# Feed-forward of an FNet + GEGLU block: 1024 tokens per first block, hidden values by way of DRAM, down projection spread over two quarters

## The chip, the cores and the metric

The kernel runs on one core of a Trainium2 chip. The metric is device time in microseconds (us): the median of several executions of the whole kernel. Engines are named as in the profile: PE (TensorE matmul) with PEld (its weight loads), DVE (VectorE), ACT (ScalarE), POOL (GpSimd), and SP, whose queue issues nearly all DMAs. Each engine works through its own queue strictly in order; an instruction that waits holds everything queued behind it.

## The reference

x has 2048 tokens of 448 values. A layer norm is followed by a Fourier mixing layer (real part of a DFT over the hidden axis and the sequence axis), added to x; then a second layer norm and a gated feed-forward with 1792 hidden values, added again:

```
h  = x + A(layernorm(x))           # a = x Wd_re^T, b = x Wd_im^T; A = Ws_re a - Ws_im b
g, u = layernorm(h) @ w_gate, layernorm(h) @ w_up
out = h + (gelu(g) * u) @ w_down
```

All arrays are float32. The kernel multiplies in float16 and splits each operand into a high and a low half (hi + lo), so that one product is three float16 products.

## The kernel before

**Stages.** The DFT over the sequence and over the hidden axis comes first and ends, on PE, at 346 us. While it runs, DVE and ACT also split all 14 blocks of gate and up weights (class `Weights`: `sums`, `split`) and store them to `w_dram`. The feed-forward starts then. Its matrix products are cut by Strassen's scheme: seven block products instead of eight, with sums of operand blocks made before (on DVE or POOL) and sums of results after.

**Gate and up (class `GateUp`, L1022).** The tokens are four quarters q of 512; by Strassen a product's moving operand has half of them, `TQ = 256` columns. For each quarter there are 14 steps f (`NF`), so t runs from 0 to 55. A step is 39 matmuls in seven products: x1, y1, x2, z1, y2, z2, y3 (L1040 to L1072), accumulated in three PSUM banks X, Y, Z. Between products other engines read a bank: ACT copies X into Y after x1 (L1043), takes u2 from Y after y1 (L1048), the gelu g1 from X after x2 (L1053), m5 from Z after z1 (L1059); DVE takes one "plus" each from Y after y2, from Z after z2 (both L1010) and from Y after y3 (L1072). `c_last` then takes a second gelu (ACT) and a multiplication on POOL (L1081). The results lie in `hh`, in SBUF, for two quarters at a time.

**Down.** d counts 56 pieces: 8 groups p of 128 tokens times 7 pieces of the hidden axis. Before piece d is used, `dn_sums` (L1121) makes sums on POOL (two) and DVE (one), `dn_hi` (L1132) two ACT copies, `dn_lo` (L1137) two DVE subtractions; then `dn_mm` runs 21 matmuls of 224 columns. After 7 pieces a `Drain` (L908) brings the group's four PSUM banks home: two copies on ACT, four additions on DVE from PSUM, eight additions on POOL (L954), a store.

**Order of the work.** Everything is ordered by hand, in the loop over t (L1260). Quarter 0 has gate and up alone, and beside it the down weights are split (`down_prep`, L967: `down_sums` on POOL, `down_hi` on ACT, `down_lo` on DVE, one n of 7 per two steps); the last two `hid_mm` of the DFT (21 matmuls each) run in it as well. From t = 14 on each step takes one d, for 42 steps; the other 14 pieces (groups 6 and 7) run in a tail after t = 55, eight of them split early (`EARLY`, L1095). The layer norm and the operand splitting of quarters 2 and 3 are laid over the steps of quarters 1 and 2 (table at L1210). Split weights are read back from `w_dram` each step (896 KB).

Of the kernel before, what the change touches and what calls it, by code (L numbers as in the profile page):

```python
# [13 lines left out]
P = 128  # L14
# [18 lines left out]
def kernel(  # L33
# [46 lines left out]
    fops = ctx.enter_context(tc.tile_pool(name="fops", bufs=1))  # L80
    dram = ctx.enter_context(tc.tile_pool(name="dram", bufs=1, space=bass.MemoryType.DRAM))
# [92 lines left out]
    hops = {}  # L174
# [3 lines left out]
    def hops_tile(q):  # L178
        hops[q] = ring.tile([P, N_OPS, 2 * P], F16, tag="ops", bufs=2, name=f"hops{q}")
# [22 lines left out]
    def down_load(n):  # L202
        wd32[n] = fops.tile([P, 4, HD], F32, tag="xn" if n % 2 else "tt", name=f"wd32_{n}")
        nc.sync.dma_start(wd32[n].rearrange("p (k c) d -> p k (c d)", k=2), w_down[n])
# [16 lines left out]

    def ffn_norm_act(q, j, h):

        tag = f"h{q}_{j}"
        mv, r = moments.pop((q, j))
        xn = fops.tile([P, 2, D], F32, tag="xn", name=f"xn_{tag}")

        nb = mv[:, :, 1]
        V.scalar_tensor_tensor(nb, mv[:, :, 0], -1.0, r, op0=ALU.mult, op1=ALU.mult)
# [57 lines left out]
    def ffn_transpose(q, j, parts):  # L287
        xs = ffn[q, j][2]
        ops = hops[q]
        for n in parts:  # L290
            s0, s1 = ((0, 8), (8, 16), (16, 22), (22, 25))[n]
            nc.sync.dma_start_transpose(ops[:, s0:s1, j * P : (j + 1) * P], xs[:, s0 * P : s1 * P])


    for q in range(2):
        hops_tile(q)
# [7 lines left out]
    class Weights:  # L304


        def __init__(self, f):
            self.f = f
            self.raw = dft.tile([P, 2, 6, P], F32, tag="raw", bufs=2, name=f"gu_raw{f}")
# [3 lines left out]
        def sums(self):  # L313
            gate, up = self.raw[:, 0], self.raw[:, 1]
            s = self.s = dft.tile([P, 10, P], F32, tag="s", name=f"gu_s{self.f}")
# [19 lines left out]
        def split(self, of_raw):  # L335
            if of_raw:
                self.w = w_tile(f"gu_w{self.f}")
            for s0, s1, src in self.parts(of_raw):
                hi_part(self.slots(0, s0, s1, src), src, W_SC)
            for s0, s1, src in self.parts(of_raw):  # L340
                lo_part(self.slots(1, s0, s1, src), src, self.slots(0, s0, s1, src), W_SC)

# [105 lines left out]
    def fast_sums(n):  # L448
        fast_s[n] = dft.tile([P, 8 * P], F32, tag="wr", bufs=5, name=f"sums{n}")
        fast_w[n] = [dft.tile([P, 2, 8 * P], F16, **place, name=f"ws{n}_{k}") for k, place in enumerate(fast_places(n))]  # L450
# [5 lines left out]

    def fast_places(n):
        ring = dict(tag="ws", bufs=6)
        return (dict(tag="raw", bufs=2), ring) if n == FAST + 2 else (ring, ring)
# [54 lines left out]
    def fast_out(n, k):  # L514

        sc = 1.0 / (X_SC * D_SC)
        if k == 1:

            e = dft.tile([P, 10, P], F32, tag="s", name=f"e{n}")
# [44 lines left out]
    def t_tile(j):  # L564
# [11 lines left out]
        if j == 7:  # L576
            return dft.tile([P, 4 * D], F16, tag="raw", bufs=2, name="t7")
# [76 lines left out]
    def wh_load(n):  # L654

        k0, k1 = WH[n]
        t = wh_raw[n] = dft.tile([P, k1 - k0, D], F32, tag="raw", bufs=2, name=f"wh_raw{n}")
# [49 lines left out]
    gu = {}  # L707

# [9 lines left out]
    for k, f in enumerate(reversed(range(NF))):  # L718
        n = (17, 20, 22, 25, 27, 30, 33, 35, 38, 40, 43, 45, 48, 50)[k]
# [72 lines left out]
    for n in range(N_STEPS):  # L792
# [89 lines left out]
        for half in range(2):  # L882
# [4 lines left out]
            for what in after.get((n, half), ()):  # L887
                what()
    z_turn(NP - 1)
    down_sums(0)  # L890

# [7 lines left out]
    gw_first = fpool.tile([P, 4, 28 * P], F16, tag="hh", bufs=2, name="gw_first")  # L899

    def gw_first_load(t, queue=nc.sync):

        gw[t] = gw_first[:, (t - 3) % 7, :]
        queue.dma_start(gw[t], w_dram[t])

    gw_first_load(4)
# [56 lines left out]
    def down_lo(n, k):  # L963
        dst, src = down_parts(n)[k]
        lo_part(wd[n][:, 1, dst], src, wd[n][:, 0, dst], W_SC)

    def down_prep(t, part=None):  # L967

        n, odd = divmod(t, 2)
        if odd and part != 1:  # L970
            if n < NC:
                down_lo(n, 1)
                if n + 2 < NC:
                    down_load(n + 2)
            if n + 1 < NC:
                down_sums(n + 1)
        elif not odd and n < NC:
            if part != 1:
                down_hi(n, 0)
                down_lo(n, 0)  # L980
            if part != 0:
                down_hi(n, 1)
# [3 lines left out]
    TQ = 2 * P  # L986

    def product(ps, q, t, a, b, first, last):

        w, ops = gw[t].rearrange("p (l o d) -> p l o d", l=2, o=14), hops[q]  # L990
# [20 lines left out]

    def ftile(tag, bufs, name, n=TQ):
        return fpool.tile([P, n], F32, tag=tag, bufs=bufs, name=name)

    hh = {}

    def f_of(t):

        q, f = divmod(t, NF)
        return f if q < 3 else f // 2 + f % 2 * (NF // 2)  # L1020

    class GateUp:  # L1022


        def __init__(self, t):
            self.t, self.name = t, f"{t}"
            self.q, self.f = t // NF, f_of(t)

            self.own = self.q > 0 or t % 2 == 0

        def bank(self, k):
            pool, tag = (ps_gu, "XYZ"[k]) if self.own else (ps_dn, f"a{k}")
            if self.q > 0 and k == 1 and self.t % 2:
                pool, tag = ps_tr, "tr"
            return pool.tile([P, 512], F32, tag=tag, name=f"p{'XYZ'[k]}_{self.name}")[:, :TQ]

        def mul(self, ps, a, b, first):
            product(ps, self.q, self.t, a, b, first, True)

        def x1(self):  # L1040
            self.X, self.Y = self.bank(0), self.bank(1)
            self.mul(self.X, "A11", "B11", True)
            A.activation(self.Y, self.X, AF.Copy)  # L1043

        def y1(self):
            self.mul(self.Y, "S2", "T2", False)
            self.u2 = ftile("u2", 2, f"u2_{self.name}")
            A.activation(self.u2, self.Y, AF.Copy, scale=SC)  # L1048

        def x2(self):  # L1050
            self.mul(self.X, "A12", "B21", False)
            self.g1 = ftile("g1", 2, f"g1_{self.name}")
            A.activation(self.g1, self.X, AF.Gelu_apprx_tanh, scale=1.0 / (X_SC * W_SC))  # L1053

        def z1(self):
            self.Z = self.bank(2)
            self.mul(self.Z, "S1", "T1", True)
            self.m5 = ftile("m5", 1, f"m5_{self.name}")
            A.activation(self.m5, self.Z, AF.Copy, scale=SC)  # L1059

        def y2(self):
            self.mul(self.Y, "S3", "T3", False)
            plus(self.hidden(1), self.Y, self.m5)

        def z2(self):
            self.mul(self.Z, "S4", "B22", False)
            self.c12 = ftile("c12", 2, f"c12_{self.name}")
            plus(self.c12, self.Z, self.u2)

        def y3(self):  # L1070
            self.mul(self.Y, "A22", "T4", False)
            V.scalar_tensor_tensor(self.hidden(0), self.Y, SC, self.g1, op0=ALU.mult, op1=ALU.mult)  # L1072

        def hidden(self, g):
            k, n = divmod(self.f, NF // 2)
            return hh[self.q][:, n, 2 * k + g, :]

        def c_last(self):
            A.activation(self.c12, self.c12, AF.Gelu_apprx_tanh, scale=1.0 / H_SC)  # L1079
            c22 = self.hidden(1)  # L1080
            G.tensor_mul(c22, c22, self.c12)  # L1081
# [6 lines left out]
    NC = NF // 2  # L1088
    dn_s, dn_w, acc_d, hr = {}, {}, {}, {}

    def dn_hid(d):
        p, n = divmod(d, NC)
        return hh[p // 2][:, n, :, p % 2 * P : (p % 2 + 1) * P]

    EARLY = [42, 43, 49, 44, 45, 50, 46, 47]  # L1095
    EARLY_AT = dict(zip((44, 46, 47, 48, 50, 51, 52, 54), EARLY))

    def dn_tile(d):

        def tile(pool, tag, bufs, n=14 * P):  # L1100
            return pool.tile([P, n], F16, tag=tag, bufs=bufs, name=f"dn_w{d}")

        if d in EARLY:
            k = EARLY.index(d)
            if k < 3:
                if k == 0:
                    dn_w["early"] = tile(ring, "ops", 2, N_OPS * 2 * P)
                w = dn_w["early"][:, k * 14 * P : (k + 1) * 14 * P]
            elif k < 6:
                w = tile(fops, ("xs", "xn", "tt")[k - 3], 1)  # L1110
# [335 lines left out]
```

## Time and profile before

| | us |
|---|---|
| median of 3 runs | 723.15 (723.01 to 725.27) |
| the profiled execution, its own time | 723.14 |
| its span, first to last instruction | 721.3 |
| first matmul of the feed-forward | 346.0 |
| first matmul of the down projection | 420.8 |
| last matmul | 717.9 |

The granted TensorE clock is 1.000 throughout. In the profile a row of the timeline has the start (us from the span's start), the duration, the engine, the source line, the operation, out<-in, the shape and a count of merged instructions; a bracket tells how long the engine sat idle before it and what released it. Rows grouped by line have the busy time and the mean ns of one instruction. Instructions of one engine follow each other a little closer than their durations say: the distance of two starts is the price, the duration is latency.

### The profile page before, as it was taken

The page shows a single profiled execution, that of the slowest core. Times are in us where ns is not written, and L with a number is a line of the kernel's source. Part 1 is how long each engine was busy: PE and PEld are TensorE (multiplying, and loading weights), DVE is VectorE, ACT ScalarE, POOL GpSimd, SP SyncE. Part 2 cuts the span into 40 slices and gives each one's busy share as a digit, 9 for nine tenths or more (in the row PEclk, how much of TensorE's full clock was granted, in tenths as well). Part 3 has the DMA queues.
Part 4 walks back from the last instruction along what each step waited for, and adds up shares of the span by engine and source line. Part 5 has one row for each costly group of instructions (what it writes and reads, how often), then busy time and mean ns, then how long its engine had stood idle before and what let it go on. Part 6 is the DMA issues. An engine that isn't in the chain of part 4 may idle for free.

```text
span 721.3 us, 14165 instructions
## 1 busy us (share of the span) xinstructions
PE 706.4 (98%) x5496; PEld 533.4 (74%) x5496; DVE 518.2 (72%) x1063; ACT 366.3 (51%) x726; POOL 190.8 (26%) x250
## 2 busy tenths in 40 slices
PE   9999999999999999999999999999999999999897
PEld 5555555555555555898778899899998999999896
DVE  7997639596959889998644567686586765667594
ACT  5776525254436655442637655554555544465431
POOL 0000000000000000000435643363453635657473
PEclk9999999999999999999999999999999999999999
DMA  8787549999999999572787325558466585444301
GB/s 268 248 249 258 130 161 272 260 333 276 250 352 287 287 292 263 190 182 92 213 318 281 130 94 157 180 180 224 156 174 178 183 222 176 160 141 165 129 20 60
DMA packets 101588, 147.70 MB, mean 205 GB/s; under 512 B 60944, under 2 KB 72336, under 8 KB 101520
## 3 DMA queue, kind: packets, MB, share of 16 engines
q1 hardware_dynamic: 101376, 145.88, 66.7%
q8 instruction: 43, 0.70, 0.4%
q10 hardware_dynamic: 144, 0.92, 0.4%
q14 instruction: 25, 0.20, 0.1%
HBM read 112.69 MB, written 20.19 MB: 184 GB/s over the span
## 4 chain that ended last, share of the span: by engine, by line
PE 90%; DVE 3%; ACT 3%; POOL 2%; DMA 1%; issue 1%; ACTq 0%; SPq 0%; DVEq 0%; POOLq 0%
PE acc L626 33%; PE pY L1000 13%; PE acc_d L1171 12%; PE y L691 9%; PE pZ L1000 8%; PE pX L1000 8%; PE acc_f L498 7%; DVE dn_w L111 2%; DMA gw<-w_dram 1%; ACT wd L107 1%; POOL hr L954 1%; ACT xn_h L231 1%; DVE wd L113 0%; POOL dn_s L1125 0%; POOL dn_s L1126 0%
## 5 line engine op out<-in xcount | busy, mean ns | idle before, releaser
L626 PE MATMUL acc<-xs,ws 128*128 128x448 f16 x1248 | 237.9, 352 | 0.3 <-DVE xs L148 0.3
L626 PEld LDWEIGHTS <-ws 128*128 128x128 f16 x1248 | 122.1, 98 | 114.3 <-issue 0.4
L1000 PEld LDWEIGHTS <-gw 128*128 128x128 f16 x1755 | 171.3, 98 | 22.4 <-issue 2.9
L1171 PE MATMUL acc_d<-wd,dn_w 128*128 128x224 f16 x1176 | 133.4, 259 | 3.3 <-ACT v L922 3.3
L1171 PEld LDWEIGHTS <-dn_w 128*128 128x128 f16 x1176 | 113.2, 98 | 6.6 <-issue 3.8
L1000 PE MATMUL pY<-hops,gw 128*128 128x256 f16 x765 | 105.2, 273 | 2.1 <-ACT u L1048 1.5
L209 POOL TENSOR_TENSOR wd_s<-wd 128x448 f32<-128x448 f32 x7 | 7.9, 1132 | 353.9 <-DVE r_h L141 342.1
L113 DVE SCALAR_TENSOR_TENSOR ws<-wr,ws 128x1024 f16<-128x1024 f32 (+2 forms) x66 | 75.0, 1139 | 6.6 <-ACT ws L107 6.6
L107 ACT ACTIVATE ws<-wr 128x1024 f16<-128x1024 f32 (+2 forms) x66 | 64.4, 980 | 29.6 <-DMA wr<-in_w_seq_dram 28.6
L1081 POOL TENSOR_TENSOR hh<-hh,c 128x256 f32<-128x256 f32 x56 | 45.5, 812 | 115.5 <-ACT c L1079 115.5
L1000 PE MATMUL pX<-hops,gw 128*128 128x256 f16 x495 | 68.8, 273 | 2.1 <-DMA gw<-w_dram 2.1
L1000 PE MATMUL pZ<-hops,gw 128*128 128x256 f16 x495 | 68.7, 273 | 0.0
L691 PE MATMUL y<-wh,z 128*128 128x448 f16 x336 | 66.2, 352 | 0.0
L1048 ACT ACTIVATE u<-pY 128x256 f32<-128x256 f32 x56 | 21.4, 382 | 79.7 <-PE pY L1000 79.6
L1125 POOL TENSOR_TENSOR dn_s<-hh 128x256 f32<-128x256 f32 x56 | 44.1, 788 | 48.9 <-DVE dn_w L111 48.8
L1010 DVE SCALAR_TENSOR_TENSOR hh<-pY,m 128x256 f32<-128x256 f32 x56 | 23.6, 421 | 43.7 <-PE pY L1000 41.3
L691 PEld LDWEIGHTS <-z 128*128 128x128 f16 x336 | 32.9, 98 | 29.6
L111 DVE TENSOR_TENSOR dn_w<-dn_s,dn_w 128x640 f16<-128x640 f32 x56 | 52.6, 940 | 1.4 <-ACT dn_w L107 1.4
L1010 DVE SCALAR_TENSOR_TENSOR c<-pZ,u 128x256 f32<-128x256 f32 x56 | 23.8, 424 | 37.3 <-PE pZ L1000 34.8
L498 PEld LDWEIGHTS <-ws 128*128 128x128 f16 x504 | 48.3, 98 | 0.9
L1126 POOL TENSOR_TENSOR dn_s<-hh 128x256 f32<-128x256 f32 x56 | 48.8, 871 | 0.0
L107 ACT ACTIVATE dn_w<-dn_s 128x640 f16<-128x640 f32 x56 | 40.8, 729 | 13.5 <-POOL dn_s L1126 7.9
(117 smaller groups left out, 874.6 us busy)
## 6 DMA issues: line engine op xcount, KB each, us to landing
gw<-w_dram SPq DMA_DIRECT2D x45, 896.0 KB, 4.7
wr<-in_w_seq_dram SPq DMA_DIRECT2D x100, 256.0 KB, 5.1
w_dram<-gu_w SPq DMA_DIRECT2D x14, 896.0 KB, 7.1
gu_raw<-in_w_gu_dram SPq DMA_DIRECT2D x28, 384.0 KB, 6.2
wr<-in_w_seq_dram SPq DMA_DIRECT2D x14, 512.0 KB, 5.6
gw_first<-w_dram SPq DMA_DIRECT2D x7, 896.0 KB, 6.2
x<-in_x_dram SPq DMA_DIRECT2D x16, 224.0 KB, 3.3
hx<-in_x_dram SPq DMA_DIRECT2D x8, 448.0 KB, 6.6
```

Of the source, the lines that this page charges most:

```text
L107: A.activation(dst, src, AF.Copy, scale=scale)
L111: V.tensor_sub(dst, src, hi)
L113: V.scalar_tensor_tensor(dst, src, scale, hi, op0=ALU.mult, op1=ALU.subtract)
L498: PE.matmul(fast_sum(n, k), fast_a(n, i, lw, a), fast_b(j, lx, b), start=j == 0 and m == 0 and k % 2 == 0, stop=j == NT // 2 - 1 and m == ...
L626: PE.matmul(acc[key][:, :D], w[:, lw, block * P : (block + 1) * P], xs[c][:, lx, :], start=c == 0 and m == 0, stop=c == NT - 1 and m == 2,)
L691: PE.matmul(y[:, :D], z[p][:, lz, k, g * P : (g + 1) * P], wh[:, lw, k, :], start=k == 0 and m == 0, stop=k == 6 and m == 2,)
L1000: PE.matmul(ps, w[:, wl, wa + ws, :], ops[:, m + ms, :], start=first and n == 0, stop=last and n == len(terms) - 1, skip_group_check=True,)
L1010: V.scalar_tensor_tensor(dst, ps, SC, other, op0=ALU.mult, op1=ALU.add)
L1081: G.tensor_mul(c22, c22, self.c12)
L1125: G.tensor_add(s[:, 0:2], t[:, 0:2], t[:, 2:4])
L1126: G.tensor_sub(s[:, 2:4], t[:, 1:4:2], t[:, 0:4:2])
L1171: PE.matmul(ps, w[:, la, a, :], wd[n][:, lb, b, :], start=n == 0 and m == 0 and opens, stop=n == NC - 1 and m == 2, skip_group_check=True,)
```

## The change

Quarters 0 and 1 become one block of 1024 tokens (`block_of(t) == 0`, t = 0 to 13) whose matmuls have 512 moving columns. Quarters 2 and 3 are blocks 1 and 2 (t = 14 to 41) with 256 columns as before. All 56 pieces of the down projection stay; the 42 that lie beside gate and up are spread over the 28 steps of blocks 1 and 2, one or two per step (`COUNT`), and 12 pieces of the last two groups are split in block 2 too (`EARLY`, one per step from t = 30), which leaves two splits to the tail.

Of the gate and up weights only six blocks (13, 12, 11, 0, 1, 2) are split during the DFT; blocks 3 to 10 (`JIT_F`) are split in steps 1 to 8 of block 0, each two steps ahead. The splitting of the down weights is moved into steps 0 to 5 (n = 0 and 1 in step 0, then one per step). The two last `hid_mm` both run in step 1. Hidden values go from a ring of three tiles (`hs`) to DRAM (`hid_dram`) and come back piece by piece (`hid_load`), except those of block 2's last two groups, which are used from SBUF. The bias of the second layer norm is a step of its own (`ffn_bias`), ahead of `ffn_norm_act`. The tiles with the tags `raw` and `s` move from the pool `dft` to a pool `prep` that stays open.

```diff
+    DFT_F = ((13, 20), (12, 25), (11, 30), (0, 45), (1, 48), (2, 50))
+    JIT_F = range(3, 11)
...
-        q, f = divmod(t, NF)
-        return f if q < 3 else f // 2 + f % 2 * (NF // 2)
+    N_GU = 3 * NF
+        self.n = 4 * P if self.block == 0 else 2 * P
...
+        def store(self):
+            k, n = divmod(self.f, NC)
+            if self.block == 0:
+                nc.sync.dma_start(hid_dram[0, n][:, :, 2 * k : 2 * k + 2], hs[self.t].rearrange(...))
+            else:
+                nc.sync.dma_start(hid_dram[1, n], hs[self.t].rearrange(...))
+    def hid_load(d):
+        p, n = divmod(d, NC)
+        hid_in[d] = fpool.tile([P, 4, P], F32, tag="hid", bufs=4, name=f"hid{d}")
+        nc.sync.dma_start(hid_in[d], hid_dram[p // 4, n][:, p % 4])
...
+    LAST = range(6 * NC, 8 * NC)
+    EARLY = {2 * NF + 2 * n + 2 + k: (6 + k) * NC + n for n in range(6) for k in range(2)}
...
+    PREPS = {0: (0, 1), 1: (2,), 2: (3,), 3: (4,), 4: (5,), 5: (6,)}
+    for t in range(NF):                      # block 0
+        w = gu.get(t + 2) if t + 2 in JIT_F else None
...
+        if prev: prev.y3()
+        if w: w.sums()                       # DVE, 4 instructions
+        cur.y1()
+        if t == 3: gelu_table()
+        if w: w.hi(True)                     # ACT, 2
+        for n in PREPS[t][:1] if t in PREPS else ():
+            down_hi(n, 0); down_lo(n, 0)     # ACT, DVE
+        cur.x2()
+        if w: w.hi(False); w.lo(True)        # ACT 2, DVE 2
+        cur.z2(); do(t, 1); cur.y2(); do(t, 2); cur.c_last()
+        if t == 1: hid_mm(NP - 1, 0)
+        prev, cur = cur, GateUp(t + 1)
+        cur.x1()
+        if w: w.lo(False)                    # DVE 2
+        for n in PREPS.get(t, ()):
+            if n == 1: down_hi(n, 0); down_lo(n, 0)
+            down_hi(n, 1)                    # ACT
+            for part in W_LO1: down_lo(n, 1, part)   # DVE 2
+            if n + 1 < NC: down_sums(n + 1)  # POOL 3
+        cur.z1()
+        if t == 1: hid_mm(NP - 1, 1); hid_add(NP - 1, 0); ffn_moments(..., 0)
+        if t == 2: hid_add(NP - 1, 1); ffn_moments(..., 1); ...; sd_last = root(...)
...
+    COUNT = (1, 2, 1, 2, 1, 1, 2, 1, 2, 1, 2, 1, 2, 2)
+    for t in range(NF, N_GU):                # blocks 1 and 2
+        now, ahead = steps[t], steps.get(t + 1, [])
...
+        dn_mm(now[0], range(0, 6)); prev.y3()
+        for d in ahead: dn_sums(d)
+        cur.y1(); cur.x2()
+        dn_mm(now[0], range(6, 13 if len(now) == 1 else 21))
+        for d in ahead: dn_hi(d)
+        cur.z2(); cur.y2(); cur.c_last()
+        for d in ahead[:1]: dn_lo(d)
+...
+        cur.x1(); ...; cur.z1()
+        for d in ahead[1:]: dn_lo(d)
+        if extra is not None: dn_sums(extra); dn_hi(extra); dn_lo(extra)
```

(Statements are joined on a line by ";" here to keep it short, and the counts of instructions are added.)

More of the change, by code (lines that the diff above doesn't have):

```diff
@@ L308, in __init__ @@
             self.f = f
-            self.raw = dft.tile([P, 2, 6, P], F32, tag="raw", bufs=2, name=f"gu_raw{f}")
+            self.raw = prep.tile([P, 2, 6, P], F32, tag="raw", bufs=2, name=f"gu_raw{f}")
             for r in range(2):
@@ L656, in wh_load @@
         k0, k1 = WH[n]
[L657 removed]
+        t = wh_raw[n] = prep.tile([P, k1 - k0, D], F32, tag="raw", bufs=2, name=f"wh_raw{n}")
         if n == 0:
@@ L1324 @@
-        do(t, 0)
-        cur.x2()
-        cur.z1()
-        dn_mm(d, range(0, 3))
-        splits = [n for n in (d + 1, EARLY_AT.get(t - 1)) if n is not None and 1 < n and (n < 6 * NC or n != d + 1)]
-        for n in splits:
-            dn_hi(n)
-        cur.y2()
+        if w:
+            w.hi(True)
+        for n in PREPS[t][:1] if t in PREPS else ():
+            down_hi(n, 0)
+            down_lo(n, 0)
+        cur.x2()
+        if w:
+            w.hi(False)
+            w.lo(True)
+        cur.z2()
@@ new lines @@
+        if t == NF - 1:
+            dn_lo(0)
+        cur.z1()
+        if t == 1:
+            hid_mm(NP - 1, 1)
+            hid_add(NP - 1, 0)
+            ffn_moments(NB - 1, 1, hp[NB - 1, 1], 0)
+            hid.close()
+            late = ctx.enter_context(tc.tile_pool(name="late", bufs=1, reuse_waits="tile"))
+            hops_tile(2)
+        if t == 2:
+            hid_add(NP - 1, 1)
+            ffn_moments(NB - 1, 1, hp[NB - 1, 1], 1)
+            h_store(NB - 1, 1)
+            sd_last = root(moments[NB - 1, 1], "h_last")
```

492 lines of the change are left out of this document (269 added, 223 removed).

## The prediction

> **What bounds the kernel now.** I read the page first: the span, the busy shares and the chain that ended last.
>
> ```profile
> span 721.3 us, 14165 instructions
> PE 706.4 (98%) x5496; PEld 533.4 (74%) x5496; DVE 518.2 (72%) x1063; ACT 366.3 (51%) x726; POOL 190.8 (26%) x250
> PE 90%; DVE 3%; ACT 3%; POOL 2%; DMA 1%; issue 1%; ACTq 0%; SPq 0%; DVEq 0%; POOLq 0%
> ```
>
> PE is the bound nearly everywhere, so the change can win only what PE loses by waiting or by overhead per matmul. For that I need the distance of two matmul starts, from the timeline (448 columns, then the row that follows it) and from the chain (256 and 224 columns; there the second number is the chain's own time), and the stage bounds from the answers on the two matmul lines.
>
> ```profile
> 361.76 4.14 PE L691 MATMUL y<-wh,z 128*128 128x448 f16 x21
> 365.73 0.82 PE L1000 MATMUL pY<-hops,gw_first 128*128 128x256 f16 x6
> 418.71 1.20 PE pY L1000 x11
> 424.19 1.34 PE acc_d L1171 x14
> L1000 PE MATMUL pX<-hops,gu_w x33: 272/273/273, 346.0 to 358.6; 128*128 128x256 f16 x33
> L1171 PE MATMUL acc_d<-wd,dn_w x1176: 256/259/260, 421.0 to 717.9; 128*128 128x224 f16 x196
> ```
>
> 3.97/21 = 0.189 us for 448 columns, 1.20/11 = 0.109 for 256, 1.34/14 = 0.0957 for 224. The feed-forward starts at 346.0. Its pure matmul time is 56 steps x 39 x 0.1092 = 238.5 (gate and up), 1176 x 0.0957 = 112.5 (down), 42 x 0.189 = 7.9 (two hid_mm), and 3.4 from the last matmul's start to the end: 346.0 + 362.3 = 708.3. The span is 721.3, so PE waits 13.0 us from 346 on; that is all that this stage has to give beside matmul overhead.
>
> **Matmuls, the one sure gain.** Steps 0 to 27 (1092 matmuls of 256 columns, 119.2 us) become 546 of 512. No row has 512 columns. From 224, 256 and 448 columns the time grows by 0.08/192 = 0.417 ns a column: 0.189 + 64 x 0.417 ns = 0.2157 us; twice a 256 is 0.218. I take 0.2157, the nearest row being 448: 117.8 us, a gain of 1.4 us (0.1 at the other end). Blocks 1 and 2, the down projection and hid_mm keep their counts. So the span is 346.0 + 117.8 + 119.2 + 112.5 + 7.9 + 3.4 = 706.8 plus whatever PE waits in the new order; 14.5 us of waiting is break-even.
>
> The Trainium skill, "TensorE: Matmul & The Clock Gate", Back-to-back issue gap, gives 216 ns by its formula for an isolated 512-column matmul, but says that a stream of weight load and matmul pairs sustains about 131 ns; by that block 0 would be 46 us shorter. The 448-column row above is such a stream and stands at 189, so the trace is against it.
>
> **DVE and POOL get in each other's way.** This carries the forecast. First what the moved steps cost, from the timeline: the split of one gate/up block in the DFT, then the down split in step 0 and a table load of ACT.
>
> ```profile
> 139.50 1.02 DVE L113 SCALAR_TENSOR_TENSOR gu_w<-gu_raw,gu_w 128x512 f16<-128x512 f32 x2
> 140.44 0.62 DVE L186 BATCH_NORM_STATS2 st_h<-hx 128x6 f32<-128x448 f32 x1
> 145.13 1.29 DVE L113 SCALAR_TENSOR_TENSOR gu_w<-gu_s,gu_w 128x512 f16<-128x512 f32 x2
> 146.45 0.56 DVE L316 TENSOR_TENSOR gu_s<-gu_raw 128x384 f32<-128x384 f32 x1
> ...
> 148.19 0.42 DVE L242 TENSOR_TENSOR tt<-xn_h 128x256 f32<-128x256 f32 x1
> ...
> 349.11 1.12 ACT L107 ACTIVATE wd<-wd_s 128x1120 f16<-128x1120 f32 x1
> 349.24 0.63 DVE L113 SCALAR_TENSOR_TENSOR wd<-wd,wd 128x448 f16<-128x448 f32 x1 [0.41 <-ACT wd L107]
> 350.26 1.32 DVE L113 SCALAR_TENSOR_TENSOR wd<-wd_s,wd 128x1120 f16<-128x1120 f32 x1 [0.40 <-ACT wd L107]
> 351.67 1.13 POOL L209 TENSOR_TENSOR wd_s<-wd 128x448 f32<-128x448 f32 x1 [5.18 <-DVE wd L113]
> ...
> 354.46 0.73 POOL L1081 TENSOR_TENSOR hh<-hh,c 128x256 f32<-128x256 f32 x1
> ...
> 383.31 1.28 ACT L128 ACT_TABLE_LOAD   x1
> ```
>
> One gate/up block is 0.94 (lo of raw, 139.50 to 140.44), 1.3 (lo of sums) and 1.74 (sums, 146.45 to 148.19) on DVE; a down n is 0.6 + 1.4 (the second in two parts now), and 2.8 on POOL (351.67 to 354.46).
>
> ```profile
> 358.04 1.31 DVE L113 SCALAR_TENSOR_TENSOR wd<-wd_s,wd 128x1120 f16<-128x1120 f32 x1
> 358.11 1.83 POOL L1081 TENSOR_TENSOR hh<-hh,c 128x256 f32<-128x256 f32 x1 [2.92 <-ACT c L1079]
> ...
> 672.86 1.34 DVE L111 TENSOR_TENSOR dn_w<-dn_s,dn_w 128x640 f16<-128x640 f32 x1
> 673.48 1.31 POOL L1126 TENSOR_TENSOR dn_s<-hh 128x256 f32<-128x256 f32 x1
> 674.12 0.95 DVE L111 TENSOR_TENSOR dn_w<-hh,dn_w 128x256 f16<-128x256 f32 x1
> ```
>
> Here POOL's multiplication takes 1.83 us instead of 0.73: it stands until DVE's 1.31 are over. Later the two go by turns, each instruction lengthened by the other's rest. So a DVE instruction with two SBUF inputs and a POOL instruction exclude each other. A DVE "plus", with one input in PSUM, doesn't take part: the next fence has it between 423 and 426 ns in all 56 steps, whatever POOL does. The Trainium skill says of this, in "GPSIMD Engine Reference", Specifications, that the SBUF interfaces are shared with VectorE, in contention with DVE instructions with two SBUF inputs; the trace agrees, by the 1.83 against 0.73, and this speaks against the change.
>
> ```profile
> L1010 DVE SCALAR_TENSOR_TENSOR c<-pZ,u x56: 423/424/426, 352.7 to 685.4; 128x256 f32<-128x256 f32 x56
> L701 DVE SCALAR_TENSOR_TENSOR hx<-y,hx 128x448 f32<-128x448 f32 x16 | 9.9, 621 | 34.4 <-PE y L691 29.4 <-DMA hx<-in_x_dram 4.9
> L107 ACT ACTIVATE gu_w<-gu_s 128x512 f16<-128x512 f32 x28 | 16.0, 617 | 0.6 <-DVE gu_s L317 0.6
> ```
>
> A plus of 512 columns: 621 + 64 x 197/192 = 687 ns, 0.6 from start to start (424 and 621 bound it below, twice 424 above). An ACT instruction of 512 columns is 0.6 (617). POOL's multiplication of 512: 0.73 and 1.13 for 256 and 448 give 2.1 ns a column, 1.27.
>
> **Block 0, step by step.** A step is 39 x 0.2157 = 8.4 us of PE.
>
> *Steps 0 to 1.* ACT gets both n = 0 and n = 1: `down_hi(1, 1)` needs POOL's sums for n = 1, and these the tile that `down_lo(0, 1)` must leave. Behind it on ACT wait m5(1) and u2(1); z2(1) on PE waits for m5. From the end of x1(1): ACT 0.5 (X to Y) and 1.0, DVE 1.4, DVE's 0.6 that slips in, POOL 2.8, ACT 1.1 and 0.6 = 8.0. PE has in that time z1, y3, y1, x2, 22 x 0.2157 = 4.7. Wait 3.3 (2.7 without the slip).
>
> *Step 1.* The second hid_mm needs the single bank that `hid_add(7, 0)` reads first, and that stands at the end of DVE's queue: from z2's start DVE has 0.8 left, then plus 0.6, sums 1.74, 0.6, 0.94, two plus 1.2, 1.3, 1.4, 0.55 = 9.1, and POOL's 2.8 + 1.27 less 0.6 beside a plus = 3.5 between them: 12.6. PE has z2, y2, hid_mm, x1, z1: 1.1 + 1.3 + 4.0 + 2.6 = 9.0. Wait 3.6 (nothing without the exclusion).
>
> *Steps 2 to 5.* DVE's two-input work per step: 1.74 + 0.6 + 0.94 + 1.3 + 1.4 = 6.0; POOL's 2.8 + 1.27 = 4.1; three plus 1.9, of which 0.6 lies beside POOL: 11.3 against 8.4, and y3 on PE waits for y2's plus behind all of it. DVE may be late by x1 and z1, 2.6 us. 4 x 2.8 - 2.6 = 8.5, in which the table loads for the last square root and for gelu (1.28 each, steps 2 and 3, ahead of u2) lie. Without the exclusion DVE needs 7.9 and only these loads remain, 2.2. Steps 6 to 13 fit: no down split, from step 9 no split at all.
>
> Waits in block 0: 3.3 + 3.6 + 8.5 = 15.4; below, 2.7 + 2.2 = 4.9 without the exclusion; above, 18.0 if DVE may not be late at all. PE's other new duties (hid stores, raw loads) ride on DMA queues whose loads are a step ahead; I cost them at nothing, and a load that comes late costs 2.15 once, as the next fence shows.
>
> **Blocks 1 and 2.** A step is 4.26 + 2.01 = 6.27 us of PE with one d, 8.28 with two.
>
> ```profile
> 635.18 0.82 DVE L111 TENSOR_TENSOR dn_w<-dn_s,dn_w 128x640 f16<-128x640 f32 x1
> 635.91 0.42 DVE L111 TENSOR_TENSOR dn_w<-hh,dn_w 128x256 f16<-128x256 f32 x1
> 636.25 0.82 DVE L111 TENSOR_TENSOR dn_w<-dn_s,dn_w 128x640 f16<-128x640 f32 x1
> ...
> 636.99 0.48 DVE L1127 TENSOR_TENSOR dn_s<-hh 128x128 f32<-128x128 f32 x2
> ...
> 638.02 0.72 POOL L1126 TENSOR_TENSOR dn_s<-hh 128x256 f32<-128x256 f32 x1
> ...
> 638.71 0.72 POOL L1081 TENSOR_TENSOR hh<-hh,c 128x256 f32<-128x256 f32 x1
> 670.68 1.29 POOL L954 TENSOR_TENSOR hr<-hr,v 128x224 f32<-128x224 f32 x2
> 678.38 0.83 PE L1000 MATMUL pX<-hops,gw 128*128 128x256 f16 x6 [2.15 <-DMA gw<-w_dram]
> ```
>
> By starts, a split of one d takes of the shared access 0.73 + 0.34 + 0.2 on DVE and 2 x 0.69 on POOL, 2.65; a multiplication 0.69; a drain 8 x 0.645 = 5.16, in two steps. Block 1 needs 21 splits, 14 multiplications, two drains, 75.6, and norm work, of 101.8: it fits. In block 2 twelve extra splits join from t = 30. Steps 33 to 40 need (13 ahead + 8 extra) x 2.65 + 8 x 0.69 + 4 x 2.58 (half drains of groups 3 and 4) = 71.5, and PE's time is 4 x 6.27 + 4 x 8.28 = 58.2: 13.3 late. What may be late unpunished is a step's extra split and drain sums, 5.2. Wait 8.1; nothing if all is absorbed, 13.3 if nothing is. Before, steps 50 to 52 have two splits, a multiplication and a quarter drain each, 7.3 against 6.27, so 3 us of lateness, and no PE wait for DVE shows there, which fits.
>
> The waits of before on the norm activations go (bias and norm are apart now), and in the tail two splits are left for six, so the drain of group 6 waits for nobody.
>
> **Sum.** 706.8 + 15.4 + 8.1 = 730.3; the profiled execution has 1.8 outside its span (723.14 against 721.3) and equals the median 723.15. Forecast 732 us, slower.
>
> **The rivals.** *A, as forecast* (0.52).
> *B, PE stays the bound* (0.24, faster): DVE and POOL slip past each other, waits 4.9 and none in block 2: 713.5. For it: before, the two share 721 us with little harm. It decides if the access is under PE's time per step; against it 11.3 against 8.4.
> *C, worse* (0.10): only the 3 us of lateness shown before are free in block 2, 10.3, and SP, whose store of a drained group waits for POOL, sends weight loads late twice, 4.3: 739.
> *D, half of it* (0.12, same): block 0 pays, block 2 absorbs: 724.
> *E, wide matmuls overlap* (0.02, faster): were a 512-column matmul as short as the 448-column row, 0.189, it would be 546 x 0.0267 = 14.6 us less than A, 717; against it the even 0.417 ns a column. With the 131 ns of the Trainium skill's TensorE page, above, it would be 686.
>
> **How the numbers follow.** Likeliest is A, 732; its own range goes from no wait in block 2 (724) to both upper bounds (706.8 + 18.0 + 13.3 + 1.8 = 740). The range of 714 to 740 takes in B's middle and C, and leaves out half of B and what lies above, under 2 in 10. A difference of about 0.3% (2.2 us) can just be told from no change. Faster 0.26 (B, E), same 0.12 (D), slower 0.62 (A, C).
>
> **What would show it.** Right: in steps 2 to 5 PE idle before pY for DVE's plus; POOL and DVE instructions at double length there; PE idle before pZ in step 1 for m5, before y for hid_add; from step 33 PE idle before acc_d for dn_lo; no wait in the tail. Wrong: gate and up at 8.4 us a step in steps 2 to 5, or no idle time on PE in block 2.

## The result, and the profile after

The changed kernel takes 744.67 us (744.26 to 745.72, 4 runs) beside 723.22 us for the kernel before on the same chip: 1.029 times as long, interval 1.027 to 1.031. The forecast was 732, with a range of 714 to 740: slower it is, but by 21 us and not by 9. From the page: the span, the busy shares, and the chain that ended last.

```profile
span 743.9 us, 13045 instructions
PE 712.6 (96%) x4952; PEld 482.1 (65%) x4952; DVE 519.4 (70%) x1024; ACT 354.7 (48%) x656; POOL 201.6 (27%) x240
PE 31%; DVE 7%; POOL 5%; ACT 3%; issue 2%; DMA 2%; SPq 0%; DVEq 0%; ACTq 0%; POOLq 0%
```

PE's busy share falls from 98% to 96%; it runs 4952 matmuls where the kernel before has 5496. The chain as printed reaches back over half the span only (its shares add up to 50%); 17 points of these are DVE's, POOL's, ACT's and the DMAs', beside 9 of 100 before. What PE waits for, from the list of PE's waits (the us in total, times, the longest; one wait before the feed-forward and one of 0.2 are left out):

```profile
PE pY L1008 <- ACT pY L1053: 6.5, 5, 2.2
PE pY L1008 <- DVE hs L1018: 5.9, 3, 2.4
PE pZ L1008 <- DVE c L1018: 3.4, 2, 3.1
PE pZ L1008 <- ACT m L1059: 3.3, 1, 3.3
PE pY L1008 <- ACT u L1064: 2.5, 6, 0.8
PE y L712 <- DVE hx L722: 2.4, 1, 2.4
PE acc_d L1214 <- DVE hs L1087: 1.4, 1, 1.4
PE acc_d L1214 <- DVE dn_w L112: 1.2, 2, 1.0
```

Three of these eight are waits that the prediction named: y3 for the plus (hs L1018), z2 for m5 (ACT m), hid_mm for hid_add (hx). It named the last one too, acc_d for dn_lo, but for block 2: there it is 0.2, and 1.0 stands in block 1's first step. The list holds no price for the clock, though. The answer by stretches of time has it (PE busy, its matmuls, then the other engines; PEclk is the granted clock):

```profile
core 0: us, PE busy (x) PEld busy (x) DVE busy (x) ACT busy (x) POOL busy (x), PEclk, DMA share, GB/s
360.00:363.50 3.50, 0.32 (x2) 0.04 (x1) 0.43 (x1) 1.59 (x3) 1.87 (x3) 0.95 0.15 60
363.50:366.60 3.10, 3.02 (x8) 1.06 (x8) 3.07 (x5) 2.29 (x6) 2.00 (x2) 0.51 0.05 16
366.60:376.40 9.80, 7.54 (x38) 3.57 (x37) 8.90 (x13) 4.00 (x6) 3.39 (x4) 1.00 0.35 120
376.40:380.00 3.60, 3.48 (x11) 1.45 (x11) 0.87 (x3) 0.00 (x0) 2.49 (x3) 0.56 0.98 334
494.40:497.00 2.60, 2.60 (x9) 1.12 (x8) 0.71 (x2) 0.00 (x0) 2.55 (x3) 0.50 0.00 0
```

In 360.0 to 363.5 PE stands; in the 3.1 us after it, it is busy all the time and gets through 8 matmuls, where 14 fit at 0.2157. The clock is half: 0.51, again 0.56 after the wait at 376, and 0.50 after the one at 493. That was in nobody's count.

To see how much is what, I take the distance of every two matmul starts from 346 us on, less what its columns cost at full clock (0.2157, 0.189, 0.109, 0.0957). An excess with PE idle in it is a wait, one without is half clock. Over 706.8, the span without waits, in us:

| | predicted | after: waits | after: half clock |
|---|---|---|---|
| block 0 | 15.4 | 13.9 | 3.1 |
| end of block 0, first step of block 1 | 0 | 4.7 | 2.9 |
| the rest (block 2 with 10.6; 1.5 at the start of the tail) | 8.1 | 12.4 | 0.1 |

37.0 in all, 706.8 + 37.0 = 743.8 for a span of 743.9. The same sums for the experiments come to 0.2 to 1.3 us under their spans; most of that is half clock in the first 7 us of the kernel, 1.4 to 2.9 from run to run, 1.8 in after.

### The profile page after: what moved, and what is told of

It is laid out like the page before. It is cut to its first block, busy times and chain, and to the rows that moved or that the text cites. A ratio compares the mean times of both kernels' runs of the same rounds, so it can differ in the third digit from the quotient of the medians.

```text
span 743.9 us, 13045 instructions
## 1 busy us (share of the span) xinstructions
PE 712.6 (96%) x4952; PEld 482.1 (65%) x4952; DVE 519.4 (70%) x1024; ACT 354.7 (48%) x656; POOL 201.6 (27%) x240
## 4 chain that ended last, share of the span: by engine, by line
PE 31%; DVE 7%; POOL 5%; ACT 3%; issue 2%; DMA 2%; SPq 0%; DVEq 0%; ACTq 0%; POOLq 0%
PE acc_d L1214 11%; PE pY L1008 9%; PE pZ L1008 5%; PE pX L1008 5%; DVE gu_w L114 2%; POOL dn_s L1173 1%; POOL dn_s L1172 1%; POOL hr L970 1%; PE y L712 1%; POOL hs L1102 1%; ACT dn_w L108 1%; DVE dn_w L112 1%; DVE wd L114 1%; DMA hid<-hid_dram 1%; DMA gu_raw<-in_w_gu_dram 1%
## 5 line engine op out<-in xcount | busy, mean ns | idle before, releaser
L1008 PEld LDWEIGHTS <-gw 128*128 128x128 f16 x1209 | 118.9, 98 | 39.2 <-issue 14.7
L1214 PE MATMUL acc_d<-wd,dn_w 128*128 128x224 f16 x945 | 106.6, 260 | 1.5 <-DVE dn_w L112 1.2
L1214 PEld LDWEIGHTS <-dn_w 128*128 128x128 f16 x945 | 91.1, 98 | 4.8 <-DVE dn_w L112 1.7
L1102 POOL TENSOR_TENSOR hs<-hs,c 128x256 f32<-128x256 f32 (+1 forms) x42 | 48.1, 1146 | 148.1 <-ACT c L1100 105.2
L1008 PE MATMUL pY<-hops,gw 128*128 128x256 f16 (+1 forms) x527 | 75.5, 287 | 8.0 <-ACT pY L1053 5.5
L1008 PEld LDWEIGHTS <-gu_w 128*128 128x128 f16 x429 | 42.1, 98 | 62.6 <-issue 14.1
L1008 PE MATMUL pZ<-hops,gw 128*128 128x256 f16 (+1 forms) x341 | 50.9, 283 | 3.4 <-DVE c L1018 3.4
L1008 PE MATMUL pX<-hops,gw 128*128 128x256 f16 (+1 forms) x341 | 51.4, 285 | 0.0
L1008 PE MATMUL pY<-hops,gu_w 128*128 128x512 f16 x187 | 44.7, 382 | 6.9 <-DVE hs L1018 5.9
L1018 DVE SCALAR_TENSOR_TENSOR c<-pZ,u 128x256 f32<-128x256 f32 (+1 forms) x42 | 21.4, 509 | 34.5 <-PE pZ L1008 34.5
L970 POOL TENSOR_TENSOR hr<-hr,v 128x224 f32<-128x224 f32 x56 | 41.5, 767 | 1.7 <-ACT v L938 1.2
```

What stands on the lines that cost most here:

```text
L970: op(x, x, m)
L1008: PE.matmul(ps, w[:, wl, wa + ws, :], ops[:, m + ms, :], start=first and n == 0, stop=last and n == len(terms) - 1, skip_group_check=True,)
L1018: V.scalar_tensor_tensor(dst, ps, SC, other, op0=ALU.mult, op1=ALU.add)
L1102: G.tensor_mul(c22, c22, self.cols(self.c12))
L1214: PE.matmul(ps, w[:, la, a, :], wd[n][:, lb, b, :], start=n == 0 and m == 0 and opens, stop=n == NC - 1 and m == 2, skip_group_check=True,)
```

## The experiments

Thirteen kernels were run. For a single execution the number is set beside 744.7 (after) or 736.1 (e1), and the evidence is its trace. Two numbers joined by + are waits and half clock of a stage.

**e1, the early hidden loads.** In the last steps of block 0 SP is asked for DMA transposes of the next operands and, behind them, for the hidden values of the first pieces. The timeline of after:

```profile
475.99 7.96 SPq L305 DMA_TRANSPOSE hops<-xs  x3
484.63 1.67 SPq L1124 DMA_DIRECT2D hid<-hid_dram  x3
490.56 0.29 DVE L1174 TENSOR_TENSOR dn_s<-hid 128x128 f32<-128x128 f32 x1 [6.74 <-DMA hid<-hid_dram]
490.77 0.68 DVE L1018 SCALAR_TENSOR_TENSOR c<-pZ,u 128x512 f32<-128x512 f32 x1
491.51 0.82 PE L1008 MATMUL pZ<-hops,gw 128*128 128x256 f16 x6 [3.08 <-DVE c L1018]
```

Three transposes hold SP's queue for 8 us. The loads leave it at 484.6 and their data come 6 us later; DVE, whose sum of piece 0 stands ahead of z2's plus in its queue, stands still for 6.74 us, and PE for 3.08. Nothing is short here but the order of one queue.

```diff
+        if t + 2 == NF:                 # a step earlier, ahead of the transposes
+            for d in (0, 1, 2): hid_load(d)
+            hr_load(0)
         do(t, 4)
...
-        if t + 1 == NF:
-            for d in (0, 1, 2): hid_load(d)
-            hr_load(0)
```

> The changed kernel with the loads of the first three pieces of hidden values (and of one residual tile) issued one step earlier, ahead of the three transposes that hold SP's queue for 8 us. If the wait at the start of block 1 (3.1 us before z1(14), 1.1 more before down, then matmuls at half the granted clock, 7.6 us together) comes from SP's order, it goes: span 743.9 - 7.6 = 736.3. If the shared access of DVE and POOL causes it, nothing moves, for POOL is idle there: 744. A halved clock that has nothing to do with the wait would leave 2.9 us: 739.

736.13 us. From its timeline and its waits:

```profile
473.98 3.04 SPq L1124 DMA_DIRECT2D hid<-hid_dram  x3
477.58 6.99 SPq L305 DMA_TRANSPOSE hops<-xs  x3
PE pZ L1008 <- DVE c L1018: 0.3, 1, 0.3
```

Waits and half clock at the block's border are 0 instead of 4.7 + 2.9 (the 0.3 in the list stands in block 2). The span is 734.4, 1.9 less than expected, since block 0, which the edit did not touch, has 13.0 + 1.8 instead of 13.9 + 3.1: the half clock after the hid_mm wait did not come this time, though the wait itself (2.4) did, and a wait of 0.8 in step 0 is missing.

**e2, no down sums on POOL.** POOL's `down_sums` for n = 1 to 6 are dropped and n = 0's used again (the sums of the down weights are left out of the result).

```diff
     def down_sums(n):
+        if n > 0:
+            wd_s[n] = wd_s[0]
+            return
```

> The changed kernel without POOL's sums of the down weights for n = 1 to 6 (those of n = 0 are used again; the down weights' sums are left out of the computation). DVE's and ACT's instructions all stay. Theory of the shared access: DVE is no longer lengthened in steps 1 to 5, so the waits for DVE's plus in steps 3 to 5 (1.6, 2.4, 1.9) shrink to under 1 in all, the wait for hid_add (2.4, with 1.7 of half clock) goes, and the wait for m5 in step 1 (3.3, with 1.5 of half clock), where ACT stands for POOL, goes too: span 729 to 732. Rival, DVE has too much work of its own: the 5.9 us in steps 3 to 5 and the 2.4 stay, only the m5 wait goes: 739.

736.56 us, between the two. The waits of PE:

```profile
PE y L715 <- DVE hx L725: 2.4, 1, 2.4
PE pY L1011 <- DVE hs L1021: 2.2, 2, 1.6
```

z2's wait for m5 is gone, the waits before y3 fall from 5.9 to 2.2, and the wait before the second hid_mm stays to the hundredth (2.38). So POOL's sums carry the first, most of the second and nothing of the third: there the theory of the exclusion falls. For the second the rows bear it out: the 74 DVE instructions that start between 380 and 430 us in after take 49.6 us there, and the same 74, paired in their order, 44.8 in e2, though nothing of DVE's was removed.

**e3, useless matmuls in the waits.** PE gets 14, 11 and 14 matmuls of 512 columns into a free bank, just ahead of z2(1), the second hid_mm and block 1's first z1.

```diff
+    def fill(n):
+        junk = ps_dn.tile([P, 512], F32, tag="a3", ...)
+        for k in range(n):
+            PE.matmul(junk, gw[cur.t][:, :P], hops[0][:, 0, :], start=True, stop=True)
```

> The changed kernel with useless matmuls of 512 columns into a bank that block 0 doesn't use, 14 before z2(1), 11 before the second hid_mm, 14 before z1(14): they fill 3.0, 2.4 and 3.0 us in which PE stood. If the half clock after these waits comes from PE having stood, it goes, 6.0 us in all, and the waits are the same with their filling: 738 to 739. If it comes from something else (load of the other engines, DMA), the half clock stays: 744.

741.22 us. The 39 matmuls are 8.4 us and fill three waits of 8.7 in all but for about 1; the half clock in block 0 and at the border is 0 instead of 3.1 and 2.9. In block 2 it came instead after a wait of 2.17 that had none in after (1.6). So half clock comes from PE's standing, but not after each wait.

**e4, the extra splits one step later.** ACT and DVE split an extra piece (those of `EARLY`) a step after its sums.

```diff
-        if extra is not None: dn_sums(extra); dn_hi(extra); dn_lo(extra)
+        if EARLY.get(t - 1) is not None: dn_hi(EARLY[t - 1]); dn_lo(EARLY[t - 1])
+        if extra is not None: dn_sums(extra)
```

> The changed kernel with the copies and subtractions of each extra split of block 2 one step after its sums on POOL; amounts are the same. In the changed kernel ACT stands for POOL right behind the sums, 1.9 to 2.3 us a time, with u2 or the X copy behind it. Theory of capacity (DVE and POOL have more work by turns than PE has time in steps 33 to 40, 71.5 against 58.2): the waits of 12.1 us in block 2 move but stay within 2 us: 742 to 745. Rival, only the order on ACT: 8 us or more go: 736 or less.

751.55 us, worse than either theory gave: block 2 and tail have 16.3 + 4.4 instead of 12.4 + 0.1, among them waits of 4.1 and 3.3 before a y1. But the edit does more than it was meant to. The sums of the extra pieces have one tile (tag `s`, a single buffer), and now the subtractions for the low half, which read this tile, come a step later, just ahead of the next sums: from 600 to 722 us POOL waits 27 us for DVE's low halves before its sums, in e1 1.7. So e4 tells nothing about the order of ACT's queue; e12 does.

**e5, the order of block 0.** On top of e1: n = 1 is split only in step 1, its second part behind z1; n = 2 to 6 a step later each; and `hid_add(7, 0)` right behind y2's plus.

```diff
-    PREPS = {0: (0, 1), 1: (2,), 2: (3,), 3: (4,), 4: (5,), 5: (6,)}
+    PREPS = {0: (0,), 2: (2,), 3: (3,), 4: (4,), 5: (5,), 6: (6,)}   # n = 1: by hand in step 1
...
+        if t == 1: hid_add(NP - 1, 0)     # ahead of w.lo(False) and the down split
         if w: w.lo(False)
...
-            hid_mm(NP - 1, 1); hid_add(NP - 1, 0)
+            hid_mm(NP - 1, 1)
```

> The early hidden loads of e1, and in block 0: ACT and DVE split the second part of n = 1 only in step 1 (behind z1), n = 2 to 6 move from steps 1 to 5 into steps 2 to 6, and hid_add(7, 0) stands on DVE right behind the plus of y2. My theory, order of the queues (z2 of step 1 waits only because both n = 0 and n = 1 stand in ACT's queue in step 0; the second hid_mm only because hid_add is last in DVE's queue): against e1's 736.1 the wait of 3.3 and its half clock of 1.7 go, and the wait of 2.4 goes; steps 2 to 5 lose nothing and step 6 gains a split, so 0 to 2 us come back: 729 to 731. Rival, capacity (the same work of DVE and POOL is only shifted, and PE meets it in steps 2 to 6): 733 to 736, with more than 6 us of waits before y3 in steps 2 to 6.

733.71 us. The total lies where the rival had it. z2(1) and the second hid_mm wait no more (`hid_add` starts at 367.2 us, as the first hid_mm ends) and the half clock behind them is gone, but the waits before y3 grow from 5.8 to 7.8, with a fourth one in step 6:

```profile
PE pY L1008 <- DVE hs L1018: 7.8, 4, 2.4
```

Block 0 is 10.2 + 1.4 beside e1's 13.0 + 1.8. Two waits were order; the third is capacity, and takes what is moved to it.

**e6, all gate and up blocks split in the DFT.** On top of e1, `JIT_F` is empty and `DFT_F` has all 14 blocks, as the kernel before had them.

> The early hidden loads of e1, and all 14 gate and up blocks split during the DFT as before the change, so that DVE has none of this in block 0. My theory (the waits before y3 in steps 2 to 5 and before the second hid_mm are DVE's load, JIT split plus down split, with POOL): these go, 5.9 + 2.4, less what the table loads cost; z2 of step 1 still waits 3.3 with half clock after it; first feed-forward matmul at 346.0 still, since the DFT hid this work before: 727 to 729. Rival 1, POOL and its down sums alone make these waits: they stay, 734 to 736. Rival 2, the split in the DFT is not free: the feed-forward starts later than 346.0 by over 1 us.

730.99 us, from its waits:

```profile
PE pZ L1006 <- ACT m L1057: 3.3, 1, 3.3
PE y L712 <- DVE hx L722: 2.4, 1, 2.4
```

No wait before y3 is left, out of 5.8. The second hid_mm waits its 2.4 all the same, which I had put to this load as well: wrong a second time. The DFT pays nothing for the eight blocks; the first matmul of the feed-forward stands at 345.8. Why hid_mm waits, the timeline of after tells:

```profile
371.38 1.46 PE L1008 MATMUL pX<-hops,gu_w 128*128 128x512 f16 x6
372.68 1.46 PE L1008 MATMUL pZ<-hops,gu_w 128*128 128x512 f16 x6
372.88 0.58 ACT L1053 ACTIVATE pY<-pX 128x512 f32<-128x512 f32 x1 [1.46 <-PE pX L1008]
373.37 1.13 ACT L108 ACTIVATE wd<-wd_s 128x1120 f16<-128x1120 f32 x1
374.53 1.39 DVE L114 SCALAR_TENSOR_TENSOR wd<-wd_s,wd 128x448 f16<-128x448 f32 x2 [0.90 <-ACT wd L108]
375.85 0.62 DVE L722 SCALAR_TENSOR_TENSOR hx<-y,hx 128x448 f32<-128x448 f32 x1
376.52 1.77 PE L712 MATMUL y<-wh,z 128*128 128x448 f16 x5 [2.38 <-DVE hx L722]
```

x1 ends at 372.9; then one after the other ACT's copy 0.5, ACT's high half 1.15, DVE's low half 1.3 and the addition 0.67, with DVE idle for 0.90 in between: 3.6 us, less the 1.3 of z1. A chain over two queues, no engine short of time. (The first two rows give the price of a 512-column matmul too: 1.30/6 = 0.217.)

**e7, fewer extra splits in block 2.** On top of e1: eight pieces split early instead of twelve, over steps 30 to 38; six splits stand in the tail.

```diff
-    EARLY = {2 * NF + 2 * n + 2 + k: (6 + k) * NC + n for n in range(6) for k in range(2)}
+    EARLY = {30: 42, 31: 49, 32: 43, 34: 50, 35: 44, 36: 51, 37: 45, 38: 52}
```

> The early hidden loads of e1, and in block 2 only eight pieces are split early instead of twelve, spread over steps 30 to 38; six splits stand in the tail. Theory, capacity of DVE and POOL in block 2 (each split takes 2.65 us of their shared access): the count of steps 30 to 40 comes out 7.6 us late at most instead of 13.3; waits of block 2 fall from 11.4 by 4 to 7, and the tail, where a piece has 2 us of PE and nothing else to split, may wait 0 to 2 us: 728 to 732. Rival, the order alone (ACT's dn_hi of the extra piece ahead of u2): waits go in proportion to the number of extras in steps 30 to 41, 8 of 12, so 4 us less, and none in the tail: 732. Rival, the tail cannot take the splits: waits of over 4 us there, 736 or more.

736.14 us, the same as e1. The waits of block 2 fall from 12.4 to 5.7, but the tail has 2.5 + 1.7 now (a drain's copy on ACT stands behind dn_hi's that are all late, since the first of them waits 6.9 us for POOL's eight additions of group 5), and block 0 drew 13.7 + 3.1 beside e1's 13.0 + 1.8. Both theories gave 4 us or more in block 2; the prices of the tail and of the clock ate it. The third, that the tail cannot take the splits, came nearest: 4.2 there, though only 2.5 of it are waits.

**e10 and e11, whose load it is in block 2.** On top of e1, either POOL's two sums of eleven extra pieces are left out (the first piece's are used again), or DVE's two subtractions (its low half is used again), so that sums or low halves are missing in the result.

```diff
+        if d == 42 or d not in EARLY.values():        # e10, in dn_sums
             G.tensor_add(s[:, 0:2], ...); G.tensor_sub(s[:, 2:4], ...)
...
+        if d != 42 and d in EARLY.values(): return    # e11, in dn_lo
```

> e1 with POOL's two sums of each extra piece left out, the first piece's being used again (it leaves sums of hidden values out): 11 x 2 x 0.69 = 15 us less on POOL in block 2. Theory, shared access: the waits of block 2, 11.4 in e1, fall to 3 or less: 727 to 729. Rival, ACT's own work (dn_hi of the extras) holds u2 and the copy of X: they stay above 8: 733 or more.

> e1 with DVE's two subtractions of each extra piece left out (the first piece's low half is used again): 11 x 1.07 = 12 us less on DVE in block 2, all of it shared access. Theory, shared access: POOL gets through sooner though nothing of its own is removed, the waits of block 2 fall from 11.4 to 2 to 6: 727 to 731. Rival, POOL's own queue alone (its sums and drains in a burst) is late: 9 or more stay: 734 or more.

731.58 and 731.41 us; the waits of block 2 and the tail's start are 4.9 and 4.1 instead of 12.4 (the totals fall by less, since block 0 drew half clock of 4.8 and 5.0 in these two, 1.8 in e1). What PE waits for from 600 us on, first in e1, then in e10, then in e11:

```profile
PE pY L1008 <- ACT pY L1053: 5.5, 3, 2.2
PE pY L1008 <- ACT u L1064: 2.5, 6, 0.8
```

```profile
PE pY L1008 <- ACT pY L1053: 2.8, 2, 1.9
```

```profile
PE pY L1008 <- ACT pY L1053: 1.9, 2, 1.4
PE pY L1008 <- ACT u L1064: 0.7, 2, 0.5
```

Twelve us taken from DVE alone free PE as much as fifteen taken from POOL alone, though the late instructions are POOL's in both: it is the one access that both share. The rows bear this out. The 92 POOL instructions that start between 600 and 704 us in e1 take 80.2 us there; the same 92 in e11, where none of them was removed, take 75.2, and their idle time falls from 24.6 to 22.5. So of the 7.1 us by which POOL is done sooner, 5 are shorter instructions, and only 2 come from what POOL waits for. The Trainium skill, "GPSIMD Engine Reference", Specifications, names that sharing; here is what it costs at the end of a chain of four queues.

**e8 and e9, all of it.** e8 is e1, e5, e6 and e7 together. e9 has besides POOL's additions of a drain 3, 3 and 2 to a step instead of 4 and 4, and those of group 5 behind the tail's last sums.

> All of it: early hidden loads, all 14 weight blocks split in the DFT, the down splits of block 0 one step later each, hid_add right behind its plus, eight early pieces in block 2. If the causes add up, the span is the count without waits, 706.8, plus the waits left in block 2 and the tail (4 to 7), plus 1.8 outside the span: 713 to 717, faster than before by 6 to 10 us (ratio 0.986 to 0.992). If the wide matmuls win nothing or the causes are one capacity that shifts from stage to stage: 720 to 728.

> e8 with POOL's additions of a drain spread 3, 3 and 2 over three steps instead of 4 and 4 over two, and in the tail the eight additions of group 5 behind the last sums (i == 5 instead of 2). Theory, POOL's bursts hold ACT's dn_hi and behind it the copy of X into Y: e8's wait of 2.3 with half clock 1.6 at 633 and its 1.75 at 667 fall by at least half, and the tail's 2.5 with half clock 1.6 goes: 712 to 715. Rival, capacity of the whole block 2: the same 4 to 5 us of waits in other steps, only the tail's 4.1 goes: 715 to 717.

e8: 718.79 us (718.02 to 720.63, 6 runs), ratio 0.993, interval 0.991 to 0.995; block 0 has 0.9 + 0, the rest 7.2 + 3.8. e9: 717.02 us (715.19 to 718.09, 6 runs), ratio 0.991, interval 0.989 to 0.993; block 0 has 0 + 0.1, the rest 6.4 + 1.7. So both are faster than the kernel before, by some 5 and 6 us, and each some 2 us above the range of its theory (e9 at the top of its rival's). Only 1.4 us of e9's gain are the wide matmuls; the rest is waiting, 13.0 in the kernel before and 6.4 + 1.8 in e9. e9's waits:

```profile
PE acc_d L1212 <- ACT v L936: 3.0, 2, 2.4
PE pY L1006 <- ACT u L1062: 1.1, 2, 0.9
PE pY L1006 <- ACT pY L1051: 0.8, 2, 0.4
```

Spreading the drains brings the wait for ACT's copy from 4.5 (e8) to 0.8. The tail's wait did not go as I expected: it only changed its reason, from ACT's queue behind dn_hi to POOL's additions themselves, which the copy must wait for.

**e12 and e13, the second piece's high half later.** What was open then: 12.1 us from 600 us on where the prediction had 8.1, by the order of ACT's queue or by load alone? On top of e1 (e12) and of e9 (e13), ACT makes the high half of a step's second piece behind the copy of X and m5.

```diff
-        for d in ahead: dn_hi(d)
+        for d in ahead[:1]: dn_hi(d)
         cur.z2()
...
         for d in ahead[1:]:
+            dn_hi(d)
             dn_lo(d)
```

> e1, and in blocks 1 and 2 ACT makes the high half of a step's second piece behind the copy of X and m5 instead of ahead of z2. Theory, slack lost in ACT's queue (the copy of X needs no sum, but stands behind a dn_hi that waits for POOL): the waits before y1 for the copy, 5.5 from 600 us on, go, and the waits of block 2 fall from 12.4 to 5 to 8, near the 8.1 of the prediction: 729 to 732. Rival, load alone (DVE and POOL are late by the same amount, and PE meets it at the next thing that needs them, u2, m5 or the piece itself): 11 or more stay, 735 or more.

> e9 with the same edit. e9's waits for ACT's copy of X are 0.8 us in all and the rest is u2 (1.1), a drain's copy (0.6) and the tail (2.4 with half clock). If ACT's order is all that is left in block 2: 1 us less, 715.5 to 717; if the second piece now comes late, the same or up to 3 us more.

e12: 735.29 us. The rest has 9.5 instead of e1's 12.4 (block 0 drew 13.7 + 2.8 this time). What PE waits for from 600 us on:

```profile
PE pY L1008 <- ACT u L1064: 5.9, 7, 1.5
PE acc_d L1214 <- DVE hs L1087: 1.4, 1, 1.4
```

The 5.5 for the copy are gone altogether, but u2, next on ACT behind a high half, grows from 2.5 to 5.9. So neither theory has it alone: 2.9 us were order, and the load stays, and looks for the next thing in the queue. Without the 1.5 at the start of the tail, which both kernels have, block 2 has 8.0 left in e12, 10.6 in e1. e13: 716.22 us (714.97 to 718.07, 6 runs), ratio 0.989, interval 0.987 to 0.991: the fastest of all by its median, not told apart from e9.

## Why the prediction was wrong

**Base and matmuls: right.** 0.217 for 512 columns against 0.2157; 706.8 closes the sum in every kernel. Rival E is out, and so are the 131 ns that the prediction names beside it.

**Block 0, steps 0 to 1: right.** z2(1) waits 3.26 for m5, forecast 3.3. The rows of after (released by POOL's last sum, in ACT's queue ahead of m5):

```profile
361.22 0.65 POOL L222 TENSOR_TENSOR wd_s<-wd 128x224 f32<-128x224 f32 x1
361.90 1.14 ACT L108 ACTIVATE wd<-wd_s 128x1120 f16<-128x1120 f32 x1 [4.22 <-POOL wd_s L222]
362.95 0.58 ACT L1059 ACTIVATE m<-pZ 128x512 f32<-128x512 f32 x1
363.58 1.01 PE L1008 MATMUL pZ<-hops,gu_w 128*128 128x512 f16 x2 [3.26 <-ACT m L1059]
```

**Step 1, hid_mm: right in place, wrong in reason.** 2.4 for 3.6. I had it from DVE's load under the exclusion, "nothing without the exclusion"; e2 and e6 take either load away and it stays, e5 turns the order and it goes. That the sizes are near each other is luck.

**Steps 2 to 5: right in kind, somewhat too large.** 5.9 against 8.5 (9.0 by its own 11.3 and 8.4), before y3 for y2's plus. e2 and e6 show that both engines' loads are in it, as the exclusion has it (49.6 against 44.8 us in e2). Block 0 as a whole, 13.9 for 15.4, is nearer than its parts: it has 1.5 of small waits before y1 that the prediction did not name.

**"I cost them at nothing": the first step that failed.** The hidden loads were not "a step ahead" of their use but behind three transposes in SP's queue. It cost 4.7, and 2.9 of half clock, instead of nothing or the 2.15 of one late load; e1 shows it. The prediction counted what each queue carries, not what stands in front of what.

**The clock: not in the sum at all.** 6.1 us of half clock in after. The kernel before never paid it from 346 us on, so the prediction priced every wait at its own length.

**Block 2: load right, path wrong, slack too generous.** The lag of 13.3 less "a step's extra split and drain sums, 5.2" was to leave 8.1; measured 10.6. The forecast looked for it before acc_d, for dn_lo; it comes before y1 instead, from the timeline of after:

```profile
653.27 3.14 POOL L970 TENSOR_TENSOR hr<-hr,v 128x224 f32<-128x224 f32 x4
656.37 0.77 POOL L1172 TENSOR_TENSOR dn_s<-hid 128x256 f32<-128x256 f32 x1
657.10 0.72 POOL L1173 TENSOR_TENSOR dn_s<-hid 128x256 f32<-128x256 f32 x1
657.78 0.91 POOL L1172 TENSOR_TENSOR dn_s<-hid 128x256 f32<-128x256 f32 x1
658.65 1.38 POOL L1173 TENSOR_TENSOR dn_s<-hid 128x256 f32<-128x256 f32 x1
660.06 0.74 ACT L108 ACTIVATE dn_w<-dn_s 128x640 f16<-128x640 f32 x1 [1.17 <-POOL dn_s L1173]
661.01 0.36 ACT L1053 ACTIVATE pY<-pX 128x256 f32<-128x256 f32 x1
661.43 0.81 PE L1008 MATMUL pY<-hops,gw 128*128 128x256 f16 x6 [2.16 <-ACT pY L1053]
```

Four drain additions and four sums go ahead on POOL, the last one at 1.38 instead of 0.72; ACT waits for it with dn_hi, and the copy of X, which needs no sum at all, stands behind dn_hi in ACT's queue. So a late drain sum is not unpunished: it makes the next piece's sums late, and through ACT the next y1. By their rows, DVE's instructions with two SBUF inputs and POOL's cover 92% of 640 to 700 us in after. e10 and e11 bear out the load, e9 the burst. The 2.5 us over the forecast go with this order: e12 takes 2.6 away by turning it. That its 8.0 is so near the 8.1 is partly luck, for they stand before y1 for u2 and nearly none before acc_d.

**Tail: nearly right.** The drain of group 6 waits for nobody in after. But a wait of 1.4 (1.5 by the starts) stands in the tail's first piece, at 714.2 us: its last matmuls need the bank that the last y3's plus reads (hs L1087), and that plus is behind the last extra piece in DVE's queue. It is gone in e11 and where the extra pieces end earlier (e7, e8, e9): order once more.

**Of the rivals,** C was nearest: slower still, by block 2 and by late loads on SP. It had the late loads with weights and behind a store.

The errors add up: -1.5 in block 0, +4.7 at the border, +4.3 in the rest (2.5 in block 2, 1.5 at the tail, 0.3 in block 1), +6.1 of clock: 13.6, from 730.3 to the span of 743.9.

## What to carry to other kernels

Moving work to another stage moves it into other queues: for each step, list what stands ahead of it in each in-order queue and what that waits for, DMA queues too; three of the five kinds of wait here (z2, hid_mm, the border) went by a change of order alone, though two of the 5.7 us of z2 and hid_mm came back before y3, where the load is. Work that sits free beside a long stage (here the weight splits, in the DFT) is only worth moving if the stage needs the relief; a gain of 1.4 us does not pay for filling two engines that share one access to above nine tenths. And price a wait of the matmul engine above two microseconds higher than its length: by the table that follows, half clock may come behind it.

## What the hardware showed

Over the fifteen traces, from 346 us on, the half clock goes by how long PE had stood (idle time just before the next matmul, and how many of such stands were followed at once by half clock):

| PE stood, us | stands | half clock after |
|---|---|---|
| 1.0 to 2.0 | 50 | 0 |
| 2.0 to 2.3 | 11 | 4 |
| 2.3 to 2.6 | 23 | 14 |
| over 2.6 | 12 | 11 |

Three times it came behind a second, shorter stand within 4 us (after, at 493.8: 3.08, then 0.95 idle, then 2.9 lost; e2: 2.49 and 0.96; e5: 1.97 and 0.60). One spell costs 1.4 to 1.7 us as a rule; the longest are the 2.9 just named and one of 2.8 in e12. The same stand in the same kernel place has it in one run and not in another (2.38 before the second hid_mm: 7 of 9). The Trainium skill, "TensorE: Matmul & The Clock Gate", Part 1, tells of a free-running window of about 3.4 us after which an idle array is gated to half: 1.7 lost at half clock is 3.4 us, which agrees, and a window that runs free would make it a matter of chance, as seen; but read as a window that is idle throughout it does not agree, as stands of 2.2 us did it four times.
